# Score tails of both heads made in the first head's step, in the banks of the transposes, where P goes by DMA

## The chip, the cores and the metric

The kernel runs on one core of a Trainium2 chip. The metric is device microseconds of one execution, the median of several runs. TensorE (PE) does the matrix products and transposes, VectorE (DVE) the search for the largest scores, ScalarE (ACT) copies out of the accumulation banks and the exponentials, GpSimd (POOL) element-wise work, and SyncE (SP) issues nearly all DMAs. The engines run their own instructions in order and wait for each other by semaphores.

## What is computed

Attention that keeps the 32 largest scores of each row, and behind it a mixing block: a real part of a two-dimensional Fourier transform, a normalisation and a two-layer network.

```python
def _attn_ref(q, k, v):                      # 8 batches, 8 heads, 576 rows, 64 wide
    scores = scale * np.matmul(q, k.transpose(0, 1, 3, 2))
    kth = np.partition(scores, -top_k, axis=-1)[..., -top_k:-top_k + 1]
    mask = scores >= kth                     # top_k = 32
    scores = np.where(mask, scores, -1000000000.0)
    attn = np.exp(scores - np.max(scores, axis=-1, keepdims=True))
    attn = attn / (np.sum(attn, axis=-1, keepdims=True) + 1e-09)
    return np.matmul(attn, v)

def _moe_ref(x, w_ch1, w_ch2):               # x: 8 x 576 x 512
    u = x + np.real(np.fft.fft(np.fft.fft(x, axis=1), axis=2))
    un = (u - mu) / np.sqrt(var + 1e-06)     # over the last axis
    return u + np.maximum(un @ w_ch1, 0.0) @ w_ch2
```

## The kernel before

**Tiles.** The 64 heads are taken as 32 pairs, four pairs to a batch. A pair has nine items (`IN_PAIR`): its 576 query rows are four blocks of 128 rows, each once for either head (e = 0 and e = 1), and one joint item (e = None) that holds the last 64 rows of both heads. There are 288 items and the main loop makes one step of each. Step i carries work of several items: the scores of item j = i + 3, the rounds of the search for items i and i + 1 on VectorE (each item has four MAX8 and three MATCH_REPLACE8 over 128 x 576), the bounds of item i on GpSimd (L431), and the mask and exponential of item i - 1.

**Scores.** An item has 576 scores a row. `scores(j, 0)`, in the step of a first head or a joint item, makes the scores against the first 512 keys: for a first head, those of both heads of the block, one product of 64 channels each (L398), into two `sp` banks, and ACT copies each into its `S` tile (L401). For a joint item they are four products of 256 keys (L383) into two banks and four copies (L390). The last 64 keys, the tails, come from `scores(j, 1)`: one product (L368) against `kt_t`, which holds the tail keys of both heads on its diagonal, so that one product serves both heads, and two copies (L372) into the tails of the two `S` tiles. For blocks, this product is made one step later, in the step of the second head; for a joint item, at the end of TensorE's fixed work in the same step. VectorE's first round of an item reads the whole `S` tile (L422).

**Banks.** The eight accumulation banks are split into `ps_s` with two (scores, tag `sp`), `ps_t` with two (tag `tp`: the transposes of queries and keys, L308, and those of P, L524), one for the attention output (L561) and three that are handed round for the rest. A tile of a tag waits until the tile two before it on that tag has been read. `sp` was shared by score products and tails.

**P by DMA.** In pairs for which `pair_by_dma` holds (pairs 4 to 30 without 7, 26 in all) P is not transposed on TensorE: ACT splits its words into two planes (L469), SP writes them to DRAM (L482), and a transposing DMA brings them back (L503). In those pairs `tp` is used by the transposes of the next pair's queries and keys alone (`prep`, at i % 9 = 0 and 5, two tiles each), with copies on ACT.

**Order.** The order on each engine is written out by the loop. In a step with such an item, ACT gets the mask of item i - 1 (L445), the two planes of item i - 2 (L469), then the copies of the fixed work, and the exponential of item i - 1 (L456). TensorE gets the list `fixed`: scores first, then transposes, then parts of the Fourier transform, and for a joint item the tails. Between the entries of `fixed`, `some` puts units from a queue: hidden units (L963) and back units (L990, L1029, L1160) of the network of an earlier batch. How many go into a step follows from `room`: the step's length (`level`) less `fixed_cost(i)`, in which the scores of a first head count 1.04, the tails 0.3 and a joint item 0.9 us.

The lines that choose the tails' place and bank:

```python
            sp = ps_s.tile(shape, F32, name=name, tag="sp") if i else bank(shape, name)   # L365
        fixed.append(lambda: scores(j - 1, 1) if e == 1 else scores(j, 0))                # L1508
        if e is None and j < N:                                                           # L1525
            fixed.append(lambda: scores(j, 1))
```

Of the kernel before, what the change touches and what calls it, by code (L numbers as in the profile page):

```python
# [9 lines left out]
F32 = mybir.dt.float32  # L10
# [63 lines left out]
def kernel(  # L74
# [46 lines left out]
    ps_s = ctx.enter_context(tc.tile_pool(name="ps_s", bufs=2, space=bass.MemoryType.PSUM))  # L121
    ps_t = ctx.enter_context(tc.tile_pool(name="ps_t", bufs=2, space=bass.MemoryType.PSUM))
# [7 lines left out]
    def bank(shape, name, hold=False):  # L130
        n = banks_free.pop(0)
        t = ps_m.tile(shape, F32, name=name, tag=f"m{n}", bufs=1)
        if not hold:
            banks_free.append(n)
            return t
        return t, lambda: banks_free.append(n)
# [157 lines left out]
    def prep(n, pair, blocks=((0, NF), (NF, NC))):  # L294

        if pair >= NPAIR:
            return 0.0
        src, got_of = nat[n, pair], qT_of if n == "q" else kT_of
        if pair not in got_of:
            got_of[pair] = attp.tile(  # L300
                [P, S if n == "q" else NF * P], F32, name=f"{n}T_{pair}", tag=f"{n}T",
                bufs=2 if n == "q" else 1
            )
        t_sb = got_of[pair]
        for c0, c1 in blocks:
            tp = ps_t.tile([P, 4, P], F32, name=f"tp{n}_{pair}_{c0}", tag="tp")
            for c in range(c0, c1):
                nc.tensor.transpose(  # L308
                    tp[:, c - c0, :], src[:, c, :, :].rearrange("p h d -> p (h d)"), ident
                )  # L310
            if c0 < NF:
                dst, got = t_sb[:, c0 * P:c1 * P], tp.rearrange("p a c -> p (a c)")[:, 0:(c1 - c0) * P]
            else:
                dst, got = t_sb[:, NF * P:], tp[:, 0, 0:TAIL]
            if n == "q":
                nc.scalar.mul(out=dst, in_=got, mul=scale)
            elif c0 < NF:
                nc.scalar.copy(out=dst, in_=got)
            else:
                for e in range(2):  # L320
                    r = slice(D * e, D * (e + 1))
                    nc.scalar.copy(out=kt_t[r, TAIL * e:TAIL * (e + 1)], in_=tp[r, 0, 0:TAIL])
        return 0.7
# [7 lines left out]
    items = [(pair, t, e) for pair in range(NPAIR) for t, e in IN_PAIR]  # L331
    N = len(items)

    def scores(i, part):

        if not 0 <= i < N:
            return 0.0
        pair, t, e = items[i]  # L340
        qT, kT = qT_of[pair], kT_of[pair]
        rows = ROWS[t]
        if part == 0:
            for n in range(1 if e is None else 2):
                Ssb[i + n] = attp.tile([P, S], F32, name=f"S_{i + n}", tag="S", bufs=6)
        q_cols = slice(P * t, P * t + rows)


        plain = (slice(0, NF * P), slice(NF * P, S))
        tails_first = (slice(TAIL, S), slice(0, TAIL))  # L350
        if e is None:
            to = [
                (Ssb[i], slice(TAIL * h, TAIL * (h + 1)), *(tails_first if h and by_dma(i) else plain))
                for h in range(2)
            ]
        else:
            to = [
                (Ssb[i], slice(0, P), *plain),
                (Ssb[i + 1], slice(0, P), *tails_first),
            ]  # L360
        if part == 1:

            copy = nc.scalar.copy if i else nc.vector.tensor_copy
            shape, name = [P, NF * P], f"sp_{i}_t"
            sp = ps_s.tile(shape, F32, name=name, tag="sp") if i else bank(shape, name)  # L365

            q_end = P * t + rows
            nc.tensor.matmul(  # L368
                sp[:, 0:P], lhsT=qT[:, q_end - P:q_end], rhs=kt_t, start=True, stop=True
            )  # L370
            for h, (s_t, r, _, tails) in enumerate(to):
                copy(out=s_t[r, tails], in_=sp[P - rows:P, TAIL * h:TAIL * (h + 1)])  # L372
            return 0.3
        if e is None and i >= PER_BATCH:

            half = NF * P // 2
            sps = [
                ps_s.tile([P, NF * P], F32, name=f"sp_{i}_{h}", tag="sp") for h in range(2)
            ]
            for g in range(2):  # L380
                for h in range(2):
                    hd = slice(D * h, D * (h + 1))
                    nc.tensor.matmul(  # L383
                        sps[h][TAIL * g:TAIL * (g + 1), 0:half],
                        lhsT=qT[hd, q_cols], rhs=kT[hd, half * g:half * (g + 1)],
                        start=True, stop=True,
                    )
            for h, (s_t, r, keys, _) in enumerate(to):
                for g in range(2):
                    nc.scalar.copy(  # L390
                        out=s_t[r, keys][:, half * g:half * (g + 1)],
                        in_=sps[h][TAIL * g:TAIL * (g + 1), 0:half],
                    )
            return 0.6
        for h, (s_t, r, keys, _) in enumerate(to):
            hd = slice(D * h, D * (h + 1))
            sp = ps_s.tile([P, NF * P], F32, name=f"sp_{i}_{h}", tag="sp")
            nc.tensor.matmul(  # L398
                sp[r], lhsT=qT[hd, q_cols], rhs=kT[hd, :], start=True, stop=True
            )  # L400
            nc.scalar.copy(out=s_t[r, keys], in_=sp[r])  # L401
        return 1.04
# [32 lines left out]
    def pair_by_dma(pair):  # L435

        return NPB <= pair < NPAIR - 1 and pair != 2 * NPB - 1

    def by_dma(i):
        return pair_by_dma(i // PER_PAIR)  # L440
# [848 lines left out]
    for c in range(2):  # L1289
        scores(0, c)  # L1290
    prep("q", 0, ((2, NF), (NF, NC)))
    scores(2, 0)


# [145 lines left out]
    def chunk_at(i):  # L1440

        for tile in (i - 4, i - 3, i - 2):
            r = tile % PER_PAIR
            if PER_BATCH <= tile < N and r in (4, 8):
                if i - tile == (4 if by_dma(tile) else 2 if tile == 2 * PER_BATCH - 1 else 3):
                    return tile // PER_PAIR, r // 8
        return None, None

    def fixed_cost(i):

        t = 0.55 if 0 <= i - 2 < N and not by_dma(i - 2) else 0.0
        if i + 3 < N:
            t += {0: 1.04, 1: 0.3, None: 0.9}[items[i + 3][2]]
        ch = chunk_at(i)[1] if i > PER_BATCH + 3 else {4: 0, 8: 1}.get((i - 3) % PER_PAIR)
        t += 0.0 if ch is None else (CW[ch] / 115.0 + 0.14 * len(CHUNKS[ch]))
        if i < N and i % PER_PAIR in (0, 5):
            t += 0.7
        return t + costs.get(i, 0.0)

    def level(i):  # L1460

        steps = range(i, next((a for a in arrivals if a > i), i + PER_BATCH))
        rest, lev = sum(u[0] for u in queue + waiting), 0.0
        while lev < 6.4 and sum(max(0.0, lev - fixed_cost(s)) for s in steps) < rest:
            lev += 0.02
        return lev
# [19 lines left out]
    i, carry = 0, 0.0  # L1486
    while i < N + 5 or plan or queue or sums:
# [11 lines left out]
        fixed, j = [], i + 3  # L1499
        e = items[j][2] if j < N else None  # L1500
# [4 lines left out]
            preps.append(lambda: prep("q", pair_of + 1))  # L1505
        if i < N and i % PER_PAIR == 5:
            preps.append(lambda: prep("k", pair_of + 1))
        fixed.append(lambda: scores(j - 1, 1) if e == 1 else scores(j, 0))  # L1508
        n_mask = 0
        fixed += preps  # L1510

# [27 lines left out]
        if i in arrivals:  # L1539
            carry = min(carry, 0.0) if i > arrivals[0] else -5.0  # L1540
            run(i, "units")
            step_us = level(i)
        room = step_us - carry - fixed_cost(i)
        cost, got = carry, 0.0
        turn(i - 3)
# [105 lines left out]
```

## Time and profile before

| | |
|---|---|
| median of 3 runs | 1889.86 us (1888.66 to 1890.06) |
| the profiled execution | 1882.96 us, of which the span is 1881.2 |
| mean granted TensorE clock | 0.955 |
| tails' products (L368) | 320 instructions in 160 pairs, median 275 ns each |
| tails' copies on ACT (L372) | 318, median 209 ns |
| score products (L398) | 528 instructions, four to a block of both heads |
| ACT copies of scores (L401, L390) | 264 of median 585 ns, 112 of median 367 ns |

Busy microseconds by stretch (a stretch of some 210 us is a batch; attention ends near 1664 us):

| stretch | PE | DVE | ACT | POOL | clock |
|---|---|---|---|---|---|
| 36 to 234 | 129.1 | 193.6 | 160.8 | 146.7 | 0.81 |
| 234 to 447 | 191.7 | 196.1 | 150.4 | 94.4 | 0.95 |
| 447 to 660 | 195.8 | 195.7 | 162.3 | 107.8 | 0.95 |
| 660 to 870 | 194.6 | 196.7 | 157.2 | 105.4 | 0.97 |
| 870 to 1080 | 201.2 | 190.9 | 157.4 | 104.3 | 0.98 |
| 1080 to 1290 | 203.6 | 193.0 | 159.3 | 106.2 | 0.98 |
| 1290 to 1500 | 204.2 | 197.9 | 162.7 | 108.9 | 0.98 |
| 1500 to 1664 | 160.3 | 147.2 | 120.1 | 84.3 | 1.00 |
| 1664 to 1881 | 212.5 | 44.9 | 42.6 | 38.7 | 1.00 |

A profile gives busy time by engine, the chain of work that ended last, groups of instructions by source line (`L368` is line 368, `sp_t<-kt,qT` says which tile is written from which) and, for idle time, the instruction that released the waiting one. PEld is TensorE's weight load, which runs beside its products. The granted clock is the share of full speed that TensorE was given.

### The profile page before, as it was taken

What the parts mean: (1) busy time and instruction counts of PE and PEld (TensorE: products, weight loads), DVE (VectorE), ACT (ScalarE), POOL (GpSimd) and SP (SyncE); (2) the same over time, 40 slices, a digit from 0 to 9 for tenths busy, and PEclk for the clock granted to TensorE, in tenths of its full rate; (3) what the DMA queues carried; (4) which work ended last, traced back from release to release, by engine and by line L of the source; (5) the groups of instructions that cost most, each with busy time, mean ns of one, the idle gap of its engine ahead of it and who ended that gap; (6) DMA issues with size and microseconds to landing.
All of it is one profiled execution on the core that took longest, in us unless ns stands there. A gap on an engine that the chain in (4) does not pass through costs nothing.

```text
span 1881.2 us, 26922 instructions
## 1 busy us (share of the span) xinstructions
PE 1713.1 (91%) x8134; PEld 1086.5 (58%) x8134; DVE 1582.7 (84%) x3301; ACT 1295.7 (69%) x3104; POOL 911.3 (48%) x1278
## 2 busy tenths in 40 slices
PE   5567699889899998989999999999999999999999
PEld 3344364364466654666456665666556655666677
DVE  7999999798899999998899998999999999862110
ACT  6878658576788778777777677777787678652100
POOL 4768643455645356354544465355544465341012
PEclk8887899899899999999999999999999999999999
DMA  5333026651468755585455854685466756440132
GB/s 167 105 96 109 24 60 171 175 138 51 118 155 212 178 125 129 149 214 131 123 144 151 215 128 121 141 229 147 125 155 180 179 133 143 121 117 6 51 110 72
DMA packets 516576, 249.16 MB, mean 132 GB/s; under 512 B 398288, under 2 KB 506448, under 8 KB 516432
## 3 DMA queue, kind: packets, MB, share of 16 engines
q1 hardware_dynamic: 515664, 247.23, 50.7%
q8 instruction: 65, 1.06, 0.2%
q14 instruction: 79, 0.65, 0.1%
q10 hardware_dynamic: 768, 0.21, 0.0%
HBM read 93.63 MB, written 84.74 MB: 95 GB/s over the span
## 4 chain that ended last, share of the span: by engine, by line
PE 66%; ACT 10%; DVE 9%; POOL 7%; issue 3%; DMA 3%; SPq 2%; POOLq 0%; DVEq 0%; ACTq 0%
PE hp L963 24%; PE cp L990 8%; PE o L561 7%; PE sp L398 5%; DVE m L422 4%; PE cw L1160 4%; DVE wk L424 4%; PE yp L752 3%; PE cv L1160 3%; PE cp L1029 3%; POOL wk L448 2%; ACT wk L469 2%; ACT wk L445 2%; PE sp_t L368 2%; ACT S L456 1%
## 5 line engine op out<-in xcount | busy, mean ns | idle before, releaser
L448 POOL TENSOR_TENSOR wk<-S,wk 128x576 f32<-128x576 f32 x288 | 406.7, 1412 | 532.5 <-ACT wk L445 509.8
L422 DVE MAX8 m<-wk 128x8 f32<-128x576 f32 x864 | 626.5, 749 | 6.1
L963 PE MATMUL hp<-unT,w 128*128 128x256 f32 (+1 forms) x2048 | 535.3, 412 | 3.8 <-ACT hT L967 2.6
L963 PEld LDWEIGHTS hp<-unT,w 128*128 128x128 f32 x2048 | 379.4, 192 | 134.5 <-issue 33.4
L424 DVE MATCH_REPLACE8 wk<-m,wk 128x576 f32<-128x576 f32 x576 | 427.4, 742 | 0.0
L469 ACT COPY wk<-S 128x576 uint16<-128x576 uint16 x468 | 288.7, 666 | 0.0
L445 ACT ACTIVATE wk<-S,nt 128x576 f32<-128x576 f32 x288 | 222.5, 773 | 92.6 <-POOL nt L431 91.8
L422 DVE MAX8 m<-S 128x8 f32<-128x576 f32 x288 | 213.9, 743 | 45.1 <-ACT S L372 45.1
L990 PE MATMUL cp<-w,hT 128*128 128x512 f32 x512 | 244.0, 613 | 0.0
L561 PE MATMUL o<-PT,v 128*64 128x256 f32 (+3 forms) x1440 | 203.9, 427 | 21.8 <-DMA PT<-planes 9.9
L967 ACT ACTIVATE hT<-hp 128x320 f32<-128x320 f32 (+1 forms) x256 | 103.4, 408 | 160.2 <-PE hp L963 159.2
L424 DVE MATCH_REPLACE8 wk<-m,S 128x576 f32<-128x576 f32 x288 | 213.5, 741 | 0.0
L456 ACT ACTIVATE S<-wk,nt 128x576 f32<-128x576 f32 x234 | 182.4, 780 | 38.3 <-POOL wk L448 37.3
L398 PE MATMUL sp<-kT,qT 64*128 64x512 f32 (+1 forms) x528 | 181.5, 684 | 12.2 <-ACT means L1348 5.1
L561 PEld LDWEIGHTS o<-PT,v 128*64 128x64 f32 x1440 | 117.0, 157 | 105.7 <-issue 33.8
L401 ACT COPY S<-sp 128x512 f32<-128x512 f32 (+1 forms) x264 | 141.5, 586 | 29.5 <-PE sp L398 28.2
L990 PEld LDWEIGHTS cp<-w,hT 128*128 128x128 f32 x512 | 92.9, 194 | 107.8 <-issue 106.0
L1105 POOL TENSOR_TENSOR hT<-hT 128x512 f32<-128x512 f32 x64 | 81.3, 1274 | 105.1 <-ACT hT L967 91.2
L431 POOL TENSOR_TENSOR nt<-m,cc 128x2 f32<-128x2 f32 x288 | 59.2, 206 | 140.3 <-DVE m L422 139.3
L368 PE MATMUL sp_t<-kt,qT 128*128 128x128 f32 x320 | 70.5, 303 | 43.3 <-ACT S L390 24.4
L368 PEld LDWEIGHTS sp_t<-kt,qT 128*128 128x128 f32 x320 | 55.2, 195 | 92.3 <-ACT S L390 32.4
L1160 PE MATMUL cw<-w,hT 128*128 128x256 f32 x448 | 105.9, 383 | 0.5 <-issue 0.4
(160 smaller groups left out, 2133.1 us busy)
## 6 DMA issues: line engine op xcount, KB each, us to landing
planes<-wk SPq DMA_DIRECT2D x208, 288.0 KB, 2.7
w<-w_parts SPq DMA_DIRECT2D x82, 512.0 KB, 4.7
space<-in_moe_w_ch_dram SPq DMA_DIRECT2D x32, 512.0 KB, 3.7
nat<-in_q_dram SPq DMA_DIRECT2D x128, 64.0 KB, 2.4
v<-in_v_dram SPq DMA_DIRECT2D x64, 128.0 KB, 2.9
out_dram<-x SPq DMA_DIRECT2D x32, 256.0 KB, 2.6
nat<-in_k_dram SPq DMA_DIRECT2D x62, 128.0 KB, 2.9
planes<-wk SPq DMA_DIRECT2D x52, 144.0 KB, 2.7
```

Of the source, the lines that this page charges most:

```text
L368: nc.tensor.matmul(sp[:, 0:P], lhsT=qT[:, q_end - P:q_end], rhs=kt_t, start=True, stop=True)
L398: nc.tensor.matmul(sp[r], lhsT=qT[hd, q_cols], rhs=kT[hd, :], start=True, stop=True)
L422: ops.append(lambda src=src, m8=m8: nc.vector.max(out=m8, in_=src))
L424: ops.append(lambda src=src, m8=m8: nc.vector.match_replace(w, m8, src, NEG))
L445: nc.scalar.activation(out=w, in_=Ssb[i], func=AF.Relu, scale=-FAR, bias=Nt[i][:, 1:2])
L448: nc.gpsimd.tensor_tensor(out=w, in0=Ssb[i], in1=w, op=ALU.subtract)
L456: nc.scalar.activation(out=Ssb[i] if by_dma(i) else w, in_=w, func=AF.Exp, bias=Nt.pop(i)[:, 0:1], accum_out=den_t[pair % 3][:, c:c + 1],)
L469: nc.scalar.copy(out=words[:, half, :], in_=src[:, half, :])
L561: nc.tensor.matmul(o[D * e:D * (e + 1), c0:c1], lhsT=vv[:, c, e, :], rhs=pt[:, NF if c == NF else (NF + 1) * e + c, c0:c1], start=(c == 0) ...
L963: nc.tensor.matmul(hp[:, 0:w], lhsT=w1[:, dt, P * it:P * (it + 1)], rhs=unT[:, dt, 0:w], start=(dt == 0), stop=(dt == NDT - 1),)
L990: nc.tensor.matmul(cp, lhsT=hT[:, it, P * n:P * (n + 1)], rhs=w2[:, it, :], start=(it == 0), stop=(it == NIT - 1),)
L1160: nc.tensor.matmul(dst, lhsT=h()[a][:, kc, :], rhs=rhs_of(kc), start=start and kc == 0, stop=kc == NK - 1, skip_group_check=True,)
```

## The change

In pairs by DMA the tails' product takes a bank of `tp` instead of `sp`, and for blocks it is issued in the first head's step, directly behind the two score products, with its two copies behind theirs on ACT. The step of the second head then has no scores work there. For joint items the place stays and only the bank changes. The planner's cost of a step goes up by 0.3 for a first head's and down by 0.3 for a second head's. Pairs 0 to 3, 7 and 31 are as before.

```diff
-            sp = ps_s.tile(shape, F32, name=name, tag="sp") if i else bank(shape, name)
+            if by_dma(i):
+                sp = ps_t.tile(shape, F32, name=name, tag="tp")
+            else:
+                sp = ps_s.tile(shape, F32, name=name, tag="sp") if i else bank(shape, name)
@@ fixed_cost
             t += {0: 1.04, 1: 0.3, None: 0.9}[items[i + 3][2]]
+            if by_dma(i + 3) and items[i + 3][2] is not None:
+                t += -0.3 if items[i + 3][2] else 0.3
@@ the main loop
-        fixed.append(lambda: scores(j - 1, 1) if e == 1 else scores(j, 0))
+        if e == 0 and by_dma(j):
+            fixed.append(lambda: scores(j, 0) + scores(j, 1))
+        elif e != 1:
+            fixed.append(lambda: scores(j, 0))
+        elif not by_dma(j):
+            fixed.append(lambda: scores(j - 1, 1))
+        else:
+            fixed.append(lambda: 0.0)
```

## The prediction

> **What bounds the kernel now.** I read the page first, then busy time by stretches, then the waits of each engine between 320 and 1600 us, then single places in order of time.
>
> ```profile
> PE 1713.1 (91%) x8134; PEld 1086.5 (58%) x8134; DVE 1582.7 (84%) x3301; ACT 1295.7 (69%) x3104; POOL 911.3 (48%) x1278
> PE 66%; ACT 10%; DVE 9%; POOL 7%; issue 3%; DMA 3%; SPq 2%; POOLq 0%; DVEq 0%; ACTq 0%
> ```
>
> The chain of waits is two thirds TensorE; the rest changes between ACT, VectorE and GpSimd. TensorE is busy 1713.1 of 1881.2 us, so any gain must be TensorE idle time or TensorE time at a reduced clock. By stretches, attention ends near 1664 us; in the batches from 234 us up to there VectorE is 90 to 94% busy and TensorE 90 to 98%; behind it TensorE alone works through the last batch (212.5 of 217 us busy), which this change doesn't touch. From 320 to 1600 us the waits are:
>
> ```profile
> PE sp_t L368 <- ACT S L390: 24.4, 16, 3.6
> PE sp_t L368 <- ACT S L401: 9.8, 8, 1.9
> PE o L561 <- DMA PT<-planes: 9.8, 3, 7.5
> ...
> PE sp L398 <- ACT S L372: 3.5, 6, 1.6
> DVE m L422 <- ACT S L372: 45.1, 21, 6.3
> ...
> ACT wk L445 <- POOL nt L431: 85.4, 64, 4.8
> ```
>
> The columns are total us, times, longest. TensorE's largest wait is that of the tails' matmul for its bank: `sp` has two banks, and the tails take the bank that ACT has not yet emptied of the scores (L401), or of the halves of a joint tile (L390). VectorE's largest wait is for the copies of the tails (L372). The last line is the root: ACT is late because it waits for GpSimd's bounds.
>
> ```profile
> 911.25 0.49 PE L368 MATMUL sp_t<-kt,qT 128*128 128x128 f32 x2 [1.65 <-ACT S L390]
> 929.81 0.49 PE L368 MATMUL sp_t<-kt,qT 128*128 128x128 f32 x2 [1.01 <-ACT S L401]
> 920.43 0.76 DVE L422 MAX8 m<-S 128x8 f32<-128x576 f32 x1 [1.98 <-ACT S L372]
> 751.74 0.49 PE L368 MATMUL sp_t<-kt,qT 128*128 128x128 f32 x2 [2.07 <-ACT S L390]
> 752.50 3.40 PE L398 MATMUL sp<-kT,qT 64*128 64x512 f32 x4 [0.28 <-ACT S L390]
> ```
>
> In order of time: start, length, instruction, and in the bracket the idle time ahead with its releaser. The granted clock is the third number from the end of these two stretches:
>
> ```profile
> 750.00:760.00 10.00, 7.99 (x16) 4.08 (x17) 9.83 (x25) 7.43 (x18) 4.33 (x16) 0.66 0.59 152
> 910.00:920.00 10.00, 8.75 (x25) 3.89 (x26) 8.31 (x16) 8.63 (x19) 8.23 (x8) 1.00 0.47 120
> ```
>
> A wait of 1.65 us left the clock at 1.00; 2.07 and 0.28 us together brought it to 0.66 over ten us, that is 3.4 us of lost TensorE time.
>
> **The change, part by part.** The 26 pairs with P by DMA have 104 first-head, 104 second-head and 26 joint tiles. Work stays: each tails' product is two instructions, 0.49 us on TensorE, and two copies of 0.21 us (the median of their 318) on ACT. For first and second heads they move one step earlier, directly behind the two score products; for joint tiles only the bank changes. No DMA is issued by the moved part and no GpSimd or SP entry is passed.
>
> *Second-head steps.* In order of time nine tails in these pairs waited for L401: 1.37 (at 279), 1.20, 1.89, 0.28, 1.20, 1.42, 1.52, 1.26, 1.01 = 11.2 us. They vanish: behind the scores the tails need a bank of `tp`, which in these pairs only the key and query transposes use. **-11.2**.
>
> *Joint tiles.* Of the 16 waits for L390 one (1.28, at 403) belongs to pair 7, which isn't by DMA. In eight, other products follow the tails: 0.75, 2.15, 3.56, 1.65, 0.24, 1.65, 0.24, 1.64 = 11.9. These vanish, except that at 700 the next scores come two us later and would then meet the same copies, some 1.3 us; **-10.6**. In the other seven (506, 752, 962, 1123, 1175, 1378, 1584) the next tile's scores follow at once, and the wait only moves to them: they need the same banks. Before, from the tails' start to the scores' end took 4.44, 4.16, 4.16, 2.77, 4.16, 3.62, 3.21 = 26.5 us. After, the first head's scores can start where the tails did, the second head's one copy pair later (0.77, as from 962.04 to 962.81), and take 1.12 (a second head alone, at 962.81): 1.89 each, 13.2 in all. **-13.3**.
>
> *Scores.* With the tails out of their ring, they no longer wait for L372: 1.10, 1.64, 0.19 outside those seven. **-2.9**.
>
> *Clock.* Stretches of 20 us around the waits at 381, 447, 523 and 700 show 0.91, so 1.8 us lost in each, 7.2. Other idle time lies beside them (1.85 us on L967 at 383), so I take half: **-3.6**. The seven above hold their clock loss in their lengths (3.40 us for four instructions that take 1.13 at 946).
>
> The Trainium skill, "TensorE: Matmul & The Clock Gate", section "HAM oscillation — how this bites in real kernels", says that only gaps above some 3.4 us throttle the array. The trace disagrees: 2.35 us were enough at 752. By the page the clock term would fall to the 1.8 us behind the one wait of 3.56 and the lengths of the seven could not shrink by faster clock, some 8 us less in the whole sum, an estimate from that page.
>
> *ACT.* 0.42 us of copies move into each first-head step, ahead of the exponential, and out of the next step. ACT is 69% busy, TensorE waited for ACT's hidden units (L967) only 2.6 us from 320 to 1600: cost 0 by that cover. Without it, 104 x 0.42 = 44 us at most, and as much relief in the next steps at the other end. I take 0, since the nearest row is the 2.6.
>
> *The transposes' banks.* Key transposes (L308) now follow tails in the ring: their second tile needs the copies of the step before. In the trace the last scores' copy ended 1.6 to 13 us before them but for some five, so the copies 0.42 later are done too. Price 5 x 0.5 = 2.5 us at most, nothing at least; I take **+1**.
>
> *The planner.* The step costs move 0.3 four times up and four times down a pair: sum 0, the same units. One unit per batch may fall on the other side of a wait: 34.45/16 = 2.15 us times 7 batches = 15 us either way. I take 0.
>
> Direct sum: 11.2 + 10.6 + 13.3 + 2.9 + 3.6 - 1 = **40.6 us**.
>
> **What is late next.** TensorE can only keep it if VectorE, ACT and GpSimd come earlier too. VectorE's 45.1 us of waits for L372 lie in these pairs, none over 6.3 us, and a first head's tails now come one step (some 5.8 us, 210/36) earlier, so almost all can go. By stage I take the smaller of both reliefs. To 600: TensorE 18 (waits 7.4 + 2.9, 2.5 of the seven, 2.7, 2.7 clock), VectorE 15.8: 15.8. From 600 to 900: 8.4 against 6.1. From 900 to 1000: 4.9 against 5.6. From 1100 on: 10.0 against 17.7. Sum 15.8 + 6.1 + 4.9 + 10.0 = 36.8. Then some comes back: ACT's 85.4 us on GpSimd stay, and at 957.5, 1170.2, 1373.3 and 1579.1 the transposes of the normalised input already wait 0.36 for ACT (L830), so TensorE reaches that place with no slack, and its lead over ACT is cut there. Nothing shows how much; the bounds are none and all. Of the chain's 34% outside TensorE half (ACT 10, GpSimd 7) belongs to engines that the change doesn't relieve directly; as VectorE's gain hastens them too, I take less than that half, a third: 36.8 x 2/3 = **24.5**.
>
> The profiled execution took 1882.96 with a span of 1881.2, so about 1858.5 for its like; the median of the runs is 6.9 higher, 1889.9 - 24.5 = **1865.4**, said as 1866.
>
> **Rivals.**
> *ACT sets the pace.* If TensorE's lead is lost at L830 in each batch, only what is gained behind that place stays, the seven: 13.3 us, 1877. For it: those 0.36 us and the 85.4. Against: VectorE's waits fall as well, and its bounds release ACT. Chance 0.17.
> *Nothing.* The waits come back in full at the next scores and at L561, which already waits 9.8 for the transposing DMA: 1890, within 4 us. For it: seven of the sixteen waits are repeated at once. Against: the nine on L401 have only other products behind them. Chance 0.09.
> *Slower: the copies crowd ACT in first-head steps.* There ACT has mask 0.78, planes 1.23, scores 1.07, exponential 0.98 and now 0.42 = 4.5 us before any hidden unit. If each step passes its 0.42 on (expo, planes, transposing DMA, L561 later) and the lighter step returns nothing, +44 against -24.5: 1909. It is slower from 24.5/0.42 = 58 of the 104 steps on. Against: L967's 2.6 us, and ACT's own waits of 85.4. Chance 0.17.
> *It doesn't do what it says*: a bank of `tp` could be as late as that of `sp`. The distances before L308 speak against it; its time is that of the rival "nothing" and its chance in that.
> The forecast has 0.57.
>
> **How the numbers follow.** What a measurement here can tell from no change is about 0.2%, 3.8 us. Faster: forecast 0.57 + ACT's pace 0.17 = 0.74; same 0.09; slower 0.17. The range: at the low end the whole direct sum with a few units of the planner, 1890 - 40.6 - 6 = 1843; at the high end half way into the slower case's loss, 1890 + 6 = 1896, which leaves some 0.12 above and 0.08 below.
>
> **What would show it.** Right: no wait of `sp_t` for L401 in these pairs and hardly one for L390; the wait of L422 for L372 below 10 us; TensorE's busy time the same within 10 us, less at a better clock; 0.91 and 0.83 stretches fewer. The seven places should show a first-head product waiting for L390 in place of the tails. Wrong: new waits of L308 for L372, of L963 for L967 over 20 us, or of L561 for its DMA that eat the gain; or VectorE's end of attention at 1664 us unmoved.

## The result, and the profile after

The changed kernel took 1876.57 us, median of 5 runs (1873.33 to 1878.86), against 1888.66 us for 5 runs of the kernel before (1881.69 to 1890.06). The ratio is 0.9949, interval 0.9933 to 0.9965: 9.6 us faster, where 24.5 were forecast. The direction was right and the size was not. All differences in us below are a ratio less one, times 1888; a half-width of 0.002 in an interval is 3.8 us.

The head of the page after, busy time by engine and the chain:

```profile
span 1874.8 us, 26903 instructions
PE 1703.8 (91%) x8134; PEld 1086.4 (58%) x8134; DVE 1583.8 (84%) x3301; ACT 1295.0 (69%) x3104; POOL 912.5 (49%) x1278
PE 55%; DVE 13%; ACT 10%; POOL 10%; issue 6%; DMA 4%; SPq 2%; POOLq 0%; DVEq 0%; ACTq 0%
```

The span fell by 6.4 us and TensorE's busy time by 9.3 us, for the same 8134 instructions. TensorE's idle time, span less busy, therefore did not fall: 168.1 before, 171.0 after. What was gained is denser work: the score products (L398 before, L401 after) are busy for 170.7 us in place of 181.5, half of the difference at the seven places of the prediction, where they take 15.2 us in place of 20.6. The mean granted clock is 0.955 in both executions. None of the 31.7 us of removed waits shows as less idle time. The chain has less TensorE and more VectorE and GpSimd than before.

Where TensorE and VectorE waited from 320 to 1600 us in the kernel after (total us, times, longest):

```profile
PE o L564 <- DMA PT<-planes: 17.0, 4, 6.6
PE o L564 <- DVE m L425: 9.3, 3, 4.3
PE sp L401 <- ACT kT L318: 9.0, 7, 2.5
PE sp L401 <- ACT S L393: 8.3, 7, 2.1
PE o L564 <- DVE x L1121: 4.5, 2, 2.8
PE tpk L308 <- ACT S L375: 3.6, 1, 3.6
PE o L564 <- ACT x L627: 2.7, 1, 2.7
PE sp_t L371 <- ACT S L404: 2.5, 1, 2.5
...
DVE x L608 <- PE tpx L604: 37.7, 17, 6.0
DVE st L844 <- POOL x L839: 11.0, 8, 2.7
DVE m L425 <- ACT S L375: 7.8, 3, 4.0
DVE rd L591 <- ACT rd L590: 7.7, 4, 2.7
```

Line numbers are three higher here from the scores on (L368 is L371, L401 is L404, L561 is L564, and L398 is L401). The tails' waits fell from 34.2 to 2.5 us and VectorE's for the tails from 45.1 to 7.8, as forecast. But all of TensorE's waits in this stretch sum to 75.8 us before and 74.1 after: the attention product waits 33.5 us in place of 19.6, the scores wait 9.0 for the key copies in place of 0.7. VectorE's waits sum to 68.8 us in place of 81.4: of the 37.3 us that it no longer waits for tails, two thirds are back at the token transposes (L604), the mixed sum (L839), the denominators (L590) and one place at L816. The token transposes were its second wait before:

```profile
DVE x L605 <- PE tpx L601: 33.5, 18, 5.8
```

Two places in order of time. First the end of one pair's scores on TensorE, then ACT at the same moment, then the joint tile:

```profile
923.76 0.71 PE L308 MATMUL tpk<-ident,nat 128*128 128x128 f32 x5
924.30 1.88 PE L993 MATMUL cp<-w,hT 128*128 128x512 f32 x4
927.34 1.13 PE L401 MATMUL sp<-kT,qT 64*128 64x512 f32 x4 [1.16 <-ACT kT L318]
928.40 0.49 PE L371 MATMUL sp_t<-kt,qT 128*128 128x128 f32 x2
```

```profile
924.90 0.78 ACT L448 ACTIVATE wk<-S,nt 128x576 f32<-128x576 f32 x1 [3.14 <-POOL nt L434]
925.58 1.23 ACT L472 COPY wk<-S 128x576 uint16<-128x576 uint16 x2
926.71 0.58 ACT L318 COPY kT<-tpk 128x512 f32<-128x512 f32 x1
```

```profile
1157.84 0.39 PE L371 MATMUL sp_t<-kt,qT 128*128 128x128 f32 x2
1160.32 2.84 PE L401 MATMUL sp<-kT,qT 64*128 64x512 f32 x4 [2.09 <-ACT S L393]
```

At 927 the reader sees a wait that has moved. TensorE no longer stops at a tail, so it reaches the next pair's scores sooner, and there it needs the key copy, which ACT makes behind a mask that itself waited 3.14 us for GpSimd. At 1160 the joint tile's tails no longer wait, and the scores behind them wait 2.09 us for the same copies (before, at 1174.72, the tails waited 2.32).

The start of one ACT instruction (the mask of each pair's first item) in both profiled executions shows where time came from. By the time of the kernel before, the kernel after is 3.6 us late at 223 us, where the change begins, 4.9 late at 446 us, 2.3 late at 553, 0.5 early at 749, 14.4 early at 1172, 7.8 early at 1375 and 6.3 early at the last item. The first 3.6 us are not the change's, since pairs 0 to 3 are as before; counted from there, 1.3 us were gained by 553, 18.0 by 1172 and 9.9 by the last item. So next to nothing was gained up to 600 us, where the forecast's stages had placed 15.8 us, and nearly half of the best lead was given back. These are two single executions.

### The profile page after: what moved, and what is told of

The parts are those of the page before. It is cut to its first block, busy times and chain, and to the rows that moved or that the text cites. A ratio compares the mean times of both kernels' runs of the same rounds, so it can differ in the third digit from the quotient of the medians.

```text
span 1874.8 us, 26903 instructions
## 1 busy us (share of the span) xinstructions
PE 1703.8 (91%) x8134; PEld 1086.4 (58%) x8134; DVE 1583.8 (84%) x3301; ACT 1295.0 (69%) x3104; POOL 912.5 (49%) x1278
## 4 chain that ended last, share of the span: by engine, by line
PE 55%; DVE 13%; ACT 10%; POOL 10%; issue 6%; DMA 4%; SPq 2%; POOLq 0%; DVEq 0%; ACTq 0%
PE hp L966 22%; PE o L564 7%; DVE wk L427 6%; DVE m L425 6%; PE sp L401 4%; PE cp L993 4%; POOL wk L451 4%; PE cw L1163 3%; PE cv L1163 3%; PE cp L1032 3%; ACT wk L448 2%; POOL fg L651 2%; PE yp L755 2%; ACT wk L472 2%; PE sp_t L371 2%
## 5 line engine op out<-in xcount | busy, mean ns | idle before, releaser
L966 PE MATMUL hp<-unT,w 128*128 128x256 f32 (+1 forms) x2048 | 529.5, 411 | 5.2 <-ACT unT L884 2.7
L564 PE MATMUL o<-PT,v 128*64 128x256 f32 (+3 forms) x1440 | 204.8, 430 | 37.9 <-DMA PT<-planes 19.5
L993 PE MATMUL cp<-w,hT 128*128 128x512 f32 x512 | 236.4, 602 | 0.0
L401 PE MATMUL sp<-kT,qT 64*128 64x512 f32 (+1 forms) x528 | 170.7, 676 | 24.2 <-ACT kT L318 9.4
L564 PEld LDWEIGHTS o<-PT,v 128*64 128x64 f32 x1440 | 117.9, 158 | 114.9 <-issue 37.0
L404 ACT COPY S<-sp 128x512 f32<-128x512 f32 (+1 forms) x264 | 141.6, 586 | 24.4 <-PE sp L401 23.3
L371 PEld LDWEIGHTS sp_t<-kt,qT 128*128 128x128 f32 x320 | 51.3, 196 | 108.9 <-issue 70.0
L527 PE MATMUL tpP<-ident,wk 128*128 128x128 f32 x216 | 40.8, 320 | 61.1 <-ACT wk L459 36.1
```

The costliest lines, as they stand in the source:

```text
L401: nc.tensor.matmul(sp[r], lhsT=qT[hd, q_cols], rhs=kT[hd, :], start=True, stop=True)
L564: nc.tensor.matmul(o[D * e:D * (e + 1), c0:c1], lhsT=vv[:, c, e, :], rhs=pt[:, NF if c == NF else (NF + 1) * e + c, c0:c1], start=(c == 0) ...
L966: nc.tensor.matmul(hp[:, 0:w], lhsT=w1[:, dt, P * it:P * (it + 1)], rhs=unT[:, dt, 0:w], start=(dt == 0), stop=(dt == NDT - 1),)
L993: nc.tensor.matmul(cp, lhsT=hT[:, it, P * n:P * (n + 1)], rhs=w2[:, it, :], start=(it == 0), stop=(it == NIT - 1),)
```

## The experiments

In the table a negative number is faster than before. "Units" are the hidden and back units of the network that the planner puts between the fixed entries of a step.

| kernel | ratio | interval | us |
|---|---|---|---|
| the change | 0.9949 | 0.9933 to 0.9965 | -9.6 |
| e1 bank alone, tails late | 1.0113 | 1.0088 to 1.0137 | +21 |
| e2 joint tiles alone | 0.9929 | 0.9913 to 0.9946 | -13.4 |
| e3 without the planner's costs | 0.9885 | 0.9867 to 0.9904 | -21.7 |
| e4 early tails, bank of `sp` | 1.0996 | 1.0969 to 1.1023 | +188 |
| e5 planner's costs alone | 0.9979 | 0.9968 to 0.9990 | -4.0 |
| e6 planner's costs halved | 0.9832 | 0.9817 to 0.9846 | -31.7 |
| e7 planner's costs reversed | 0.9890 | 0.9873 to 0.9908 | -20.8 |
| e8 blocks alone | 0.9993 | 0.9976 to 1.0009 | -1.3 |
| e9 the change, units held | 0.9903 | 0.9879 to 0.9926 | -18.3 |
| e10 old tails, units of e6 | 0.9911 | 0.9884 to 0.9938 | -16.8 |
| e11 e6, keys early | 0.9819 | 0.9787 to 0.9850 | -34.2 |
| e12 e6, bounds first | 0.9775 | 0.9746 to 0.9804 | -42.5 |
| e13 before, bounds first | 0.9959 | 0.9943 to 0.9975 | -7.7 |
| e14 the change, bounds first | 0.9885 | 0.9866 to 0.9903 | -21.7 |
| e15 e9, bounds first | 0.9861 | 0.9841 to 0.9880 | -26.2 |
| e16 e11 and e12 together | 0.9791 | 0.9770 to 0.9812 | -39.5 |
| e17 e9, tails' products twice | 0.9984 | 0.9968 to 1.0000 | -3.0 |
| e18 e9, tails' copies twice | 1.0025 | 1.0010 to 1.0040 | +4.7 |

**The parts of the change: e1 to e4.** The first theory was that ACT's pace gives all waits back ("pace"); the rival, that the planner's shift of units ate the gain ("order").

e1 keeps only the bank:

```diff
-            sp = ps_s.tile(shape, F32, name=name, tag="sp") if i else bank(shape, name)
+            if by_dma(i):
+                sp = ps_t.tile(shape, F32, name=name, tag="tp")
+            else:
+                sp = ps_s.tile(shape, F32, name=name, tag="sp") if i else bank(shape, name)
```

> Of the change only the bank: in the pairs by DMA the tails take a bank of tp, at their old place in the second head's step, planner as before. Theory 'pace': what TensorE gains by waiting less comes back at the next product that needs ACT (L401 on the key copies, L561 on the transposing DMA and on VectorE), because ACT, late by GpSimd, sets the pace; only denser scores (both heads' products side by side) and a better clock stay. Then the bank alone gives nearly all that the whole change gave (-9.6 us): -6 to -12, with TensorE's idle time from 320 to 1600 us within 5 us of before. Rival 'order': the planner's shifted units and the earlier place ate a gain of 20 us or more; then the bank alone gives -20 or better.

It was 21 us slower than before, which neither theory had. TensorE's first two waits of that kernel:

```profile
PE tpk L308 <- ACT S L375: 23.6, 11, 6.7
PE tpq L308 <- ACT S L375: 22.3, 11, 8.2
```

Left in the second head's step, the tails stand directly ahead of the transposes of keys and queries in the ring of `tp`, and those wait for copies that ACT makes in the same step. The earlier place is what makes the bank usable.

e2 takes the bank for joint tiles alone (`if by_dma(i) and e is None`); the units stand exactly as before.

> Of the change only the joint tiles' tails in a bank of tp; blocks as before. The prediction's sum gave the joint tiles 10.6 + 13.3 of 40.6 us. Theory 'pace': the seven places where the next scores follow at once keep their denser scores, the rest comes back: -3 to -8. Rival 'order': -14 or better, as nothing is reordered here.

It gave -13.4 us, between the two. Its waits from 320 to 1600 us, TensorE's then VectorE's:

```profile
PE sp_t L371 <- ACT S L404: 11.8, 9, 2.3
PE sp L401 <- ACT S L393: 11.1, 8, 2.1
...
DVE m L425 <- ACT S L375: 44.6, 20, 6.3
DVE x L608 <- PE tpx L604: 25.7, 14, 4.6
```

VectorE waits 44.6 us for the tails, as before, and the kernel is no slower than the whole change, in which this wait is 7.8 (the 3.8 us between the two are inside the noise).

e3 is the whole change without the planner's costs:

```diff
-            if by_dma(i + 3) and items[i + 3][2] is not None:
-                t += -0.3 if items[i + 3][2] else 0.3
```

> The whole change without the planner's two costs, so that the units between the scores fall as they did before. Theory 'pace': like the whole change, -6 to -13 against before. Rival 'order': the shift of units cost the difference to the forecast, so -20 or better.

-21.7 us: the rival "order" was right and "pace", as it was put, wrong. Two lines of bookkeeping that issue no instruction cost 12 us, give or take 5. The units do not quite fall as they did before, though: of the 666 numbers of units explained under e9 below, 48 differ from the kernel before, because the 0.3 us of the tails' product are now spent a step earlier.

e4 has the early place with the old bank (`sp = ps_s.tile(...)` in all pairs).

> The whole change but for the bank: the tails are made behind the scores in the first head's step, in a bank of sp. The tails then wait in each of 104 steps until ACT has emptied the first head's scores of the same step. Both theories: slower than before. If TensorE's waits could be made good elsewhere, by little (0 to +30 us); if each step waits the 1.2 us of the former waits or more, +100 us and above, and the bank is what makes the earlier place possible.

+188 us, 1.8 us for each of 104 steps: the tails wait for copies of the same step (the line numbers of this kernel are those of the kernel before).

```profile
PE sp_t L368 <- ACT S L401: 148.0, 83, 7.0
```

**The place of the units: e5 to e7, e9 and e10.** Is a shift of units bad in itself, or does any shift scatter the time?

e5 is the kernel before with the two lines of the planner.

> The kernel before with nothing but the planner's two costs (+0.3 for a first head's step, -0.3 for a second head's in the pairs by DMA); the tails stay. Theory 'order' as it now stands (the shift of units, which the prediction took as 0 with ends of 15 us, costs some 12 us by itself): +6 to +16 against before. Rival 'scatter' (any shift of units moves the time by several us, up or down): any value from -10 to +10, and no relation to the 12 us. Rival 'coupled' (the shift only hurts together with the early tails): within 3 us of before.

-4.0 us, not +12: such a shift isn't bad by itself. The rival "coupled" (within 3 us) is inside the interval and not excluded. e6 and e7 have the whole change with `-0.15 ... else 0.15` and `0.3 ... else -0.3`.

> The whole change with the planner's costs halved (+0.15 and -0.15). If the cost of the shift grows evenly with it, between the whole change and the one without costs: -12 to -20 against before, about -16. Rival 'scatter': anywhere from -5 to -27.

> The whole change with the planner's costs of opposite sign (-0.3 for a first head's step, +0.3 for a second head's), so that more units stand in first heads' steps. If the cost grows evenly with the shift: -22 or better, up to -33. Rival 'scatter': worse than -22 as likely as better.

-31.7 and -20.8 us. For costs of +0.3, +0.15, 0 and -0.3 the change gives -9.6, -31.7, -21.7 and -20.8: no slope, but a scatter of 22 us. It is wider than the rival "scatter" had said: -31.7 lies outside its -5 to -27.

e9 takes the planner out: the number of units behind each entry of `fixed`, 666 numbers, is written out as the kernel before had it, and so the tails move alone. 129 of those numbers differ in the change. The new line takes as many units as the list says:

```diff
-        while queue and got + queue[0][0] / 2 <= limit:
+        for _ in range(int(placed.pop(0))):
             got += one_unit()
```

> The whole change with every unit of the queue in exactly the place that it had in the kernel before (the planner's choices written out as a list). It shows the moved tails by themselves. Theory 'order' (the mechanism is worth about half of the direct sum of 40.6 us, and the whole change lost the rest by where its units fell): -15 to -28. Rival 'pace' (the waits come back whatever the units do): -5 to -12, like the whole change.

-18.3 us: this is what the mechanism is worth at the old places. The change with its own places gives half of that, 8.7 us less with an uncertainty of some 5. e10 has the old tails and the places of e6, by such a list.

> The tails as before, with every unit in the place that it has with halved costs (that kernel gave -32 us). If the place of units is worth its share alone: -6 to -14, and -32 is a sum of that and of the tails' -20. If it only helps with the new tails: within 5 us of before.

-16.8 us with no change to the tails at all, somewhat more than expected. With the tails' -18.3 it makes -35, near e6's -31.7. For the places of the change itself no such sum can be made: the old tails were never run with them. e5 comes nearest (52 of its 666 numbers differ from those of the change), and its -4.0 with -18.3 would make -22 against the -9.6 measured.

The traces narrow down where the change loses against e9. By the start of the same mask as above, e9 goes from 8.7 us early at 1172 us of the kernel before to 9.9 at 1375 and 14.3 at the last item. The change goes from 14.4 to 7.8 between the first two, and e5 from 9.9 to 2.3. So the change and e5, with much the same places of units but different tails, both lose some 7 us in this one batch, where e9 gains 1.2. Each is one execution.

**Which part of the tails: e8.** Blocks alone, without the planner's costs (`if by_dma(i) and e is not None`, the rest as in e3).

> The change for blocks alone (both heads' tails in the first head's step, in a bank of tp), without the planner's costs; joint tiles as before. The prediction's direct sum for blocks is 11.2 + 2.9 and the larger part of 3.6 for the clock, 16 us. Joint tiles alone gave -13, the whole without costs -22. If the parts add: -7 to -12, about half of the direct sum, as with the joint tiles. If VectorE's waits for the tails (45 us before, only blocks relieve them) were worth their length, -20 or better. If blocks only bring waits elsewhere: within 3 us of before.

-1.3 us, no difference. TensorE's largest wait in it, and VectorE's:

```profile
PE sp_t L371 <- ACT S L393: 20.2, 14, 2.5
...
DVE x L608 <- PE tpx L604: 42.1, 20, 7.0
DVE rd L591 <- ACT rd L590: 11.8, 6, 2.8
DVE st L844 <- POOL x L839: 10.2, 8, 2.8
DVE m L425 <- ACT S L375: 7.3, 3, 4.0
```

VectorE's wait for the tails is down to 7.3 us and the time hasn't moved: what was 45 us at L372 stands at L604, L590 and L839. The growth at these three is 28.5 of the 37.8 us. Its units are those of e3, 48 numbers away from before, so a few us either way remain; e9 less e2, both with the units of before, gives the blocks 4.9 us with an uncertainty of 5.4, and e3 less e8, both with the same units, gives the joint tiles 20.4 in place of e2's 13.4. What is clear is that most of the gain comes from the joint tiles.

**Whether the moved waits matter: e11 and e12.** Both start from e6. e11 makes the first 512 key transposes one step earlier, at the same places of the units (the edit in part: the second step's `prep` then makes the rest alone):

```diff
+        if e == 0 and by_dma(j) and i % PER_PAIR == 4 and by_dma(i):
+            fixed.append(
+                lambda: scores(j, 0) + scores(j, 1) + prep("k", pair_of + 1, ((0, NF),))
+            )
```

> The kernel with halved costs and the same places of the units, but the transposes of the next pair's keys (L308, the first 512) moved from the second head's step into the first head's step before it, behind the tails. The waits of the scores for the key copies (7.0 us from 320 to 1600 in that kernel, 0.7 before the change) then go. If waits that the change moved are still worth their length: -4 to -8 beside the kernel with halved costs, that is 0.979 to 0.981 of before. If TensorE's lead over ACT only finds the next wait: within 2 us of it, 0.982 to 0.984.

The 7.0 us of waits for the key copies are gone, but all of TensorE's waits in that stretch sum to 62.3 us against 61.6 in e6, and the ratio is 0.9819, in e6's interval: in the trace TensorE only reached the next wait. The times alone don't exclude a gain of a few us, since e11's interval reaches from 0.9787 to 0.9850. In the change the same sum is 74.1 us, so the places of e6 spare TensorE 12 us of waits. e12 makes GpSimd's bounds ahead of the folds:

```diff
+        bounds(i)
         run(i, "pool0")
         some_sums(max(2.1 - planned, 0.0))
-        bounds(i)
```

> The kernel with halved costs, with GpSimd making an item's bounds (L434) ahead of the folds and sums of the same step, not behind them. ACT's masks waited 77 to 86 us for the bounds in all kernels so far. If ACT's lateness by GpSimd is what bounds TensorE's lead, the waits of ACT for the bounds fall by half and the time by 5 us or more, to 0.980 of before or less. If not, within 3 us of the kernel with halved costs. If the folds, now later, hold up the Fourier transform, slower than it by up to 15 us.

11 us better than e6, and the fastest kernel of the study. ACT's waits in e12, 80.9 us for the bounds in e6:

```profile
ACT S L459 <- POOL wk L451: 56.6, 50, 10.9
...
ACT wk L448 <- POOL nt L434: 22.0, 22, 1.9
```

**Was the gain cut by ACT's lateness behind GpSimd? e13 to e16.** e13 to e15 are the kernel before, the change and e9, each with the edit of e12; e16 has it on e11.

> The kernel before with GpSimd's bounds ahead of the folds and sums of the same step; tails and units as before. Theory 'coupled' (TensorE's lead over ACT is cut by ACT's lateness, so relieving ACT helps most where the tails no longer tie TensorE to it): 0 to -8 us. Rival 'separate': -9 to -15 as with the new tails at halved costs.

> The whole change with bounds first. Coupled: more than 12 us better than the change alone, -22 or better against before. Separate: -15 to -22.

> The change with the units held in their places of before (-18 us) and bounds first. Coupled: its distance to e13 is clearly more than 18 us, 24 or more. Separate: 14 to 22.

> Halved costs, early key transposes and bounds first together. With bounds first the waits for the key copies are only 1.3 us, so nothing is left for the early transposes: within 4 us of the kernel with halved costs and bounds first, 0.975 to 0.980 of before.

Bounds first gives 7.7 us with the old tails and 7.9 with the new (e15 less e9), and the tails give 18.3 with late bounds and 18.5 with early ones (e15 less e13). The theory "coupled" fell: ACT's lateness behind GpSimd costs some 8 to 12 us, but is not what cut the tails' gain. e14 is 12 us better than the change, on the border of what was set for "coupled", yet at places of its own. e16 is as expected no better than e12.

**What a microsecond is worth: e17 and e18.** Both are e9 with work added at the same places: the tails' product issued twice, or each of its copies.

> Units held, new tails, and each of the 130 tails' products in the pairs by DMA made twice: two more instructions of 128 columns each time, by the row of the hidden units (16 x 8 instructions of 320 columns in 34.45 us, 0.84 ns a column) 0.21 us more for each pair of instructions and column pass, 0.22 x 2 = 0.43 in all, 56 us. If TensorE sets the pace alone: +45 to +60 beside e9. If it is worth about the share that the removed waits were worth (18 of 31): +25 to +40. If others set the pace: below +15.

> Units held, new tails, and each of the 260 copies of the tails in the pairs by DMA made twice on ACT: 260 x 0.21 = 55 us more of ACT. If ACT sets the pace in a part of the steps: +15 to +40 beside e9. If ACT's time hardly counts: below +8. A theory in which ACT alone set the pace would give +45 or more.

The price in e17's expectation was too high. In order of time the tails take 0.71 us for four instructions, against 0.49 for two, so 130 x 0.22 = 29 us were added (the line's busy time rose from 77.1 to 106.9 us). From e9:

```profile
933.20 0.49 PE L371 MATMUL sp_t<-kt,qT 128*128 128x128 f32 x2
```

From e17:

```profile
935.74 0.71 PE L372 MATMUL sp_t<-kt,qT 128*128 128x128 f32 x4
```

The time rose by 15.3 us, 0.53 of what was added. The bounds that were set beside the price of 56 us shrink with it: TensorE alone would be 23 to 31 us and the share 13 to 21. In e18 ACT's busy time rose from 1294.1 to 1345.4 us, and the time by 23.0, 0.45 of it:

```profile
PE 1709.5 (91%) x8134; PEld 1093.3 (58%) x8134; DVE 1584.4 (84%) x3301; ACT 1345.4 (71%) x3364; POOL 910.8 (48%) x1278
```

TensorE is 91% busy and ACT 69 to 71%, and a microsecond of either counts for about half (0.53 with an uncertainty of 0.19, and 0.45 with 0.10). No engine alone sets the pace in this stretch.

## Why the prediction was wrong

- **The waits to be removed** were read rightly. Of the 11.2 us at second heads all but one went. The 1.89 us at 381 us were miscounted: that tail belongs to pair 7, and the wait stays there (2.5 us). The joint tiles' waits went, and those with scores right behind them moved to these (L393, 8.3 us with one of 0.2 elsewhere). The scores at the seven places took 1.67 to 1.89 us at four, as the sum allowed, and 2.15 to 2.84 at three where the clock was lowered: 15.2 us in all, not 13.2.
- **Where they come back** was named in part. One third was taken for it, the page's shares of the chain being all the working behind it. With units held the tails give 18.3 us of a direct sum of 40.6, which is 0.45; joint tiles alone 13.4 of 23.9, 0.56; added TensorE work counts for 0.53. Why about half arrives was not taken apart further. The step "Of the chain's 34% outside TensorE half ... a third" kept 0.60 and was 6 us too high. The waits for the key copies (9.0 us), the largest new one on ACT, weren't on the list; the growth at L561 stood only in a rival and among the signs of being wrong.
- **The smaller of both reliefs by stage** failed as a method. VectorE's 45 us for the tails weren't a relief to be had: e8 takes 38 us of them away and gains nothing, e2 leaves them and gains 13. Up to 600 us the stages had 15.8 us, before the third was taken off, and the profile shows next to none.
- **The planner** is the step that failed most. It was taken as 0, with ends of 15 us either way. The change with its own places gives -9.6 and with the places of before -18.3, so its places cost 8.7 us (uncertain by 5); without its two costs it gives -21.7. The ends of 15 were of the right size (e10 shows 16.8 for other places alone), and the value within them is what a reading of sums can't give: the planner's costs add to 0, the places don't. The step "sum 0, the same units ... I take 0" was thus mis-sized by 8.7 us, and the share above by 6.2; together they are the 14.9 us between -24.5 and -9.6, by the way they were measured.
- **The transposes' banks** were taken as +1 and cost 3.6 us in one wait (L308 for L375). That held only for the early place: e1 shows 46 us for the late one.
- **ACT's copies** were taken as free and the 0.42 us moved, not added; e18 shows that ACT's time isn't free when added.
- **The clock** was to give 3.6 us and more at the seven places. In the two profiled executions its mean is the same, 0.955: 0.85 before and 0.84 after up to 320 us, ahead of most of the change, and 0.971 and 0.975 from 320 to 1600 us, which would be 5 us of TensorE's time. With one execution each this isn't settled. The fall of TensorE's busy time by 9.3 us can't show it either, since the score products, which wait less within themselves, make 10.8 us less.
- **The rivals.** "ACT sets the pace" named 1877 us and the time came out at 1876.6, but that is chance, not its mechanism: the waits at L830 stay at 0.36 us in each of four batches, before and after, and relieving ACT didn't change what the tails give. "Nothing" and "slower" didn't come; "doesn't do what it says" was excluded by the waits.

What stays open: which of the moved units costs the 8.7 us, some 7 of them between 1172 and 1375 us, and what the attention product's waits (33.5 us, half on the transposing DMA, the rest on VectorE and ACT) are worth. Neither was tried by itself. Whether the places act together with the tails, or only add to them, is open too: e6, e9 and e10 fit a plain sum, and the places of the change were not run with the old tails.

## What to carry to other kernels

A wait removed from the busiest engine was worth about half its length here, where several engines stop each other in turn; add a known amount of work to each and see what share of it arrives, before the sum is believed. Where a planner places filler, hold its choices fixed, by a list, when a change is measured: here the placing alone moved the time by 17 to 22 us, as much as the change or more, and a kernel may be judged by the luck of its fillers. The fastest version found takes the change with halved costs and GpSimd's bounds ahead of its folds (e12, ratio 0.9775, interval 0.9746 to 0.9804; e16 lies inside it).

## What was not expected of the hardware

A wait of 2.09 us was enough to lower TensorE's clock: behind it, at 1160.32, four score instructions took 2.84 us. At 954.22, where two of the four also started later than the others but the clock stayed at 1.00, they took 1.89. That row, and two stretches of the kernel after, the granted clock third from the end:

```profile
954.22 1.89 PE L401 MATMUL sp<-kT,qT 64*128 64x512 f32 x4 [0.38 <-ACT S L393]
1140.00:1160.00 20.00, 17.86 (x101) 10.99 (x101) 16.67 (x37) 17.82 (x41) 12.33 (x13) 1.00 0.67 163
1160.00:1180.00 20.00, 19.68 (x70) 10.60 (x71) 19.77 (x41) 15.35 (x38) 7.92 (x23) 0.83 0.63 164
```

0.83 of 20 us are 3.4 us lost at one wait of 2.09. A wait of 1.73 at 751.19 was enough too (0.66 from 750 to 760 us), while the prediction's row of 1.65 left the clock at 1.00. Where a wait has moved and is longer where it arrives, it can therefore cost more than its length: the tails at 1583.65 before had waited 0.60 us at a clock of 1.00, while the scores at 1575.62 after wait 2.09, and from 1570 to 1590 us the clock is 0.91, which is 1.8 us lost.
